# Where the first chunk's gate is held between its steps: SBUF in place of PSUM

## The chip, the cores and the metric

The kernel runs on one core of a Trainium2 chip. The metric is the device time of one execution in microseconds (us); the time of a kernel is the median of its timed runs. TensorE is called PE here (its weight loads PEld), VectorE is DVE, ScalarE is ACT, GpSimd is POOL, SyncE is SP. SBUF is the on-chip working memory, PSUM the memory that PE writes its results to; DVE and ACT reach both, POOL only SBUF.

## The reference

Sparse attention over 8 batches, 8 heads, 576 positions of 64 features, then a feed-forward layer of 4608 tokens (512 to 2048 to 512) with a quadratic gate.

```
scores = scale * q @ k.T; masked: heads 0-3 to the last 32 positions, heads 4-7 to a stride of 32
attn   = exp(scores - max); attn = attn / (attn.sum + 1e-9); x = attn @ v
h = x @ w_in                                 # 4608 x 2048
g = where(h >= 1, h, where(h <= -1, 0, (h + 1)**2 / 4))
out = g @ w_out                              # 4608 x 512
```

## The kernel before

The feed-forward layer goes over nine chunks `c` of 512 tokens, and in each chunk over 16 blocks `f` of 128 hidden features. For each block `up(c, f)` makes the hidden activations with 12 matmuls of 128x512 into one PSUM bank, the tile `h` (two such banks take turns). `gate(c, f)` turns them into the gate value g and splits it in two parts for the second product, a rounded high part `gh` and the remainder `gl`. `down(c, f)` multiplies both with the block's output weights, 12 matmuls into four PSUM banks. `down` of a block comes after the `up` of two blocks later, because gates wait in the list `pend`.

The gate is max(h, 1) or the square, whichever is smaller: ACT computes `u = relu(0.5 h + 0.5)` from PSUM into SBUF (L549), squares it in place (L550), DVE takes `min(max(h, 1), u)` (L554), then `gh` is a rounding copy of the result and `gl` the result minus `gh` (L559). In chunks 1 to 8 ACT makes `gh` (L556); in chunk 0 DVE makes it (L558). The tile `u` has one buffer, so L549 of a block has to wait until the block before has done with it.

Chunk 0 has much else to do at the same time. Weights arrive as 64-bit integers and are brought to floating point by all three engines: ACT `conv_a` (L178, L181), DVE `conv_b` (L186), POOL `conv_c` (L191), ACT `conv_d` (L197), and DVE `conv_e` (L201), which writes the low half of the weights. The attention of batch 1 is woven in between: `s` scores (PE L302), `m` masking (DVE L353), `x` row maximum (DVE L364), `a` subtraction (POOL L368), `e` exponential (ACT), `q` sum (DVE L379), `r` reciprocal (DVE L391) and scaling (POOL L392), `f` transposes (PE L405), `d` or `c` copy out of PSUM (L415, on DVE for `d`), `v` product with the values (PE L459), `h` and `l` into the feed-forward input (L500, L504).

The order on every engine is written out by hand (`manual_schedule`); nothing reorders it. For chunk 0 the table `STEPS` says what stands before `up`'s follow-up, before the gate, inside it (the call `between`) and behind it, and `halves` says which weight halves are converted around which gate: the conversion of (f + 2, 0), the input weights of two blocks later, and of the output weights of this block in the first gates.

```
STEPS = {2: ("s0", "", "m0 x0", "a0"), 3: ("s1", "e0 q0", "p0 m1 x1", "a1 r0"), 4: ("", "e1 q1", "p1", "r1"),
         5: ("f0", "", "d0", ""), 6: ("s2", "", "m2 x2", "a2"), 7: ("v0", "e2 q2", "p2 h0 l0", "r2"),
```

Of the kernel before, what the change touches and what calls it, by code (L numbers as in the profile page):

```python
# [23 lines left out]
def tile_sparse_attention_then_ffn(  # L24
# [518 lines left out]
    def gate(c, f, between=lambda: None):  # L543

        hp = o_ps.pop((c, f))
        gh = g_p.tile([P, CH], F32R, tag="gh", name=f"gh_{c}_{f}")
        gl = g_p.tile([P, CH], F32R, tag="gl", name=f"gl_{c}_{f}")
        u = g_p.tile([P, CH], F32, tag="u", bufs=1, name=f"u_{c}_{f}")
        nc.scalar.activation(u, hp, AF.Relu, bias=half, scale=0.5)  # L549
        nc.scalar.activation(u, u, AF.Square)  # L550
        between()

        g = u if (c, f) == (0, 0) else hp
        nc.vector.scalar_tensor_tensor(out=g, in0=hp, scalar=1.0, in1=u, op0=ALU.max, op1=ALU.min)  # L554
        if c:
            nc.scalar.copy(gh, g)  # L556
        else:
            nc.vector.tensor_copy(gh, g)  # L558
        nc.vector.tensor_tensor(out=gl, in0=g, in1=gh.bitcast(F32), op=ALU.subtract)  # L559
        return gh, gl  # L560
# [44 lines left out]
    with tc.manual_schedule():  # L605
# [36 lines left out]
        for c in range(NCH):  # L642
            b = need[c + 1] if c + 1 < NCH and need[c + 1] > need[c] else None
            go = attention(b, lambda u, kind, n: "a") if b is not None else None
            for f in range(NF):
                if c or f > 1:
                    up(c, f)
                pe, pre, mid, post = (LATER if c else STEPS).get(f, ("",) * 4) if b is not None else ("",) * 4
                if pe:
                    go(pe)  # L650
                if c == 0:
                    start_w(*halves[f])
                if pre:
                    go(pre)
                pend.append((c, f, gate(c, f, lambda: mid and go(mid))))
                if c == 0:
                    end_w(*halves[f])
                    if f == 9:
                        for i in range(2):
                            load_piece(NF - 2, i)  # L660
                        for i, k in ((0, 0), (0, 1), (1, 0)):
                            load_piece(NF - 1, i, k, o_p, "ob", 2)
                    if f == NF - 4:
                        load_piece(NF - 1, 1, 1, of=2)
                    if f == NF - 3:
                        fetch_qk(2, 0)
                if post:
                    go(post)
                n = 2 if 0 < c and (c, f) < (NCH - 1, NF - 1) else 1
                if len(pend) > 2:  # L670
                    down(*pend[:n])
                    del pend[:n]
# [61 lines left out]
```

## Time and profile before

| what | before |
|---|---|
| median of 3 timed runs | 881.38 us (881.37 to 883.25) |
| the profiled execution, its own time | 883.73 us |
| span of the profiled execution | 881.9 us |
| PE busy over the span | 872.9 us (99%) |
| PEld busy | 710.3 us (81%) |
| DVE busy | 384.6 us (44%) |
| ACT busy | 398.0 us (45%) |
| POOL busy | 114.7 us (13%) |

The profile comes from one execution. Its span runs from the first to the last recorded instruction; 1.8 us of the execution's own time lie outside of it. A busy share is an average over the whole span, and chunk 0 takes only its first part, so what the change does is read in that part.

### The profile page before, as it was taken

To read this page: it belongs to the slowest core of one execution; us is meant where nothing else is said; L and a number is where in the kernel's file an instruction comes from. 1 tells how busy PE (TensorE), PEld (TensorE's weight loads), DVE (VectorE), ACT (ScalarE), POOL (GpSimd) and SP (SyncE) were. 2 spreads that over 40 slices of the span, in tenths; PEclk is the share of its full clock that TensorE was granted. 3 is DMA by queue.
4 is the path that set the end of the run, shared out by engine and by line. 5 is a ranking of instruction groups with operands and counts; after the bars stand their busy time and mean duration, and the time that the engine had idled before them with its cause. 6 is when DMAs were issued, how large, how long until landed. Compare 5 with 4: busy or idle time off the path is not lost.

```text
span 881.9 us, 17353 instructions
## 1 busy us (share of the span) xinstructions
PE 872.9 (99%) x7253; PEld 710.3 (81%) x7253; DVE 384.6 (44%) x709; ACT 398.0 (45%) x732; POOL 114.7 (13%) x136
## 2 busy tenths in 40 slices
PE   8999999999999999999999999999999999999998
PEld 6788888888888888887888888888888888888886
DVE  5899854443453434434344345333453322222221
ACT  5889953434434443334434343444333433343333
POOL 6354411100120002100110011100210000000000
PEclk8999999999999999999999999999999999999999
DMA  9917331422232322421241223321222000000001
GB/s 354 405 65 242 114 121 61 140 59 60 105 100 81 83 70 72 125 64 62 81 145 52 67 105 94 87 82 49 76 82 60 33 29 1 0 35 14 1 0 48
DMA packets 41646, 77.61 MB, mean 88 GB/s; under 512 B 8800, under 2 KB 22112, under 8 KB 41568
## 3 DMA queue, kind: packets, MB, share of 16 engines
q1 hardware_dynamic: 41568, 76.50, 26.8%
q8 instruction: 57, 0.93, 0.4%
q14 instruction: 21, 0.17, 0.1%
HBM read 59.18 MB, written 17.30 MB: 87 GB/s over the span
## 4 chain that ended last, share of the span: by engine, by line
PE 95%; DMA 1%; ACT 1%; DVE 1%; SPq 1%; issue 0%; ACTq 0%; DVEq 0%
PE o L570 44%; PE h L540 44%; PE xp L459 3%; PE sc L302 3%; DMA qk<-in_qk_s 1%; PE tp L405 1%; SPq L443 0%; DMA pT<-there 0%; ACT u L549 0%; ACT u L550 0%; DMA there<-t 0%; DVE xTl L504 0%; DVE h L554 0%; SPq L237 0%; ACT gh L556 0%
## 5 line engine op out<-in xcount | busy, mean ns | idle before, releaser
L540 PE MATMUL h<-xTh,w 128*128 128x512 f32 x1152 | 373.2, 391 | 0.4 <-DVE u L554 0.4
L570 PE MATMUL o<-w,gh 128*128 128x512 f32 x1152 | 359.5, 393 | 0.1
L554 DVE SCALAR_TENSOR_TENSOR h<-h,u 128x512 f32<-128x512 f32 x143 | 100.0, 699 | 377.1 <-ACT u L550 377.0
L540 PEld LDWEIGHTS h<-xTh,w 128*128 128x128 f32 x1152 | 216.3, 188 | 46.6 <-DVE u L554 0.8
L570 PEld LDWEIGHTS o<-w,gh 128*128 128x128 f32 x1152 | 213.4, 188 | 45.3 <-ACT gh L556 0.6
L540 PE MATMUL h<-xTl,w 128*128 128x512 f32 x576 | 224.5, 390 | 0.4 <-DVE xTl L504 0.4
L570 PE MATMUL o<-w,gl 128*128 128x512 f32 x576 | 224.9, 390 | 0.0
L549 ACT ACTIVATE u<-h,half 128x512 f32<-128x512 f32 x144 | 99.1, 688 | 269.6 <-PE h L540 268.6
L559 DVE TENSOR_TENSOR gl<-h,gh 128x512 fp32r<-128x512 f32 x143 | 98.9, 692 | 84.6 <-ACT gh L556 83.7
L570 PEld LDWEIGHTS o<-w,gl 128*128 128x128 f32 x576 | 108.1, 188 | 25.7 <-DVE gl L559 0.6
L540 PEld LDWEIGHTS h<-xTl,w 128*128 128x128 f32 x576 | 108.1, 188 | 22.9 <-DVE xTl L504 1.1
L556 ACT CAST gh<-h 128x512 fp32r<-128x512 f32 x128 | 75.2, 587 | 100.1 <-DVE h L554 100.1
L550 ACT ACTIVATE u<-u 128x512 f32<-128x512 f32 x144 | 91.0, 632 | 4.6
L368 POOL TENSOR_TENSOR pr<-pr,st 128x768 f32<-128x768 f32 (+3 forms) x31 | 36.3, 1172 | 322.8 <-DVE st L364 307.6
L392 POOL TENSOR_TENSOR pr<-pr,st 128x648 f32<-128x648 f32 (+3 forms) x30 | 35.2, 1173 | 119.3 <-DVE st L391 118.4
L191 POOL TENSOR_TENSOR raw<-raw 128x512 uint32<-128x512 uint32 (+1 forms) x34 | 35.0, 1047 | 37.9 <-DVE raw L186 23.4
L504 DVE TENSOR_TENSOR xTl<-xp,xTh 128x216 fp32r<-128x216 f32 (+8 forms) x94 | 35.7, 442 | 6.0 <-ACT xTh L500 6.0
L383 ACT ACTIVATE st<-st 128x12 f32<-128x12 f32 (+2 forms) x32 | 6.8, 211 | 67.5 <-DVE st L379 67.4
L459 PEld LDWEIGHTS xp<-pT,v 64*64 64x64 f32 (+2 forms) x1760 | 29.0, 138 | 10.1 <-issue 8.2
L302 PEld LDWEIGHTS sc<-qk 64*32 64x32 f32 (+1 forms) x1856 | 25.9, 117 | 12.1 <-issue 10.1
L459 PE MATMUL xp<-pT,v 64*64 64x32 f32 (+2 forms) x1760 | 32.3, 224 | 1.5 <-DMA pT<-there 0.8
L500 ACT CAST xTh<-xp 128x216 fp32r<-128x216 f32 (+8 forms) x94 | 31.1, 459 | 6.0 <-DVE xTl L504 3.5
(56 smaller groups left out, 348.3 us busy)
## 6 DMA issues: line engine op xcount, KB each, us to landing
raw<-in_w SPq DMA_DIRECT2D x30, 512.0 KB, 9.6
qk<-in_qk_s SPq DMA_DIRECT2D x16, 604.0 KB, 4.9
qk<-in_qk_l SPq DMA_DIRECT2D x16, 576.0 KB, 4.8
out<-ob SPq DMA_DIRECT2D x35, 256.0 KB, 2.0
v<-in_v_l SPq DMA_DIRECT2D x21, 384.0 KB, 4.0
there<-t SPq DMA_DIRECT2D x96, 48.0 KB, 1.7
pT<-there SPq DMA_DIRECT2D x12, 384.0 KB, 3.0
v<-in_v_s SPq DMA_DIRECT2D x7, 384.0 KB, 4.4
```

The source lines that it names most:

```text
L302: nc.tensor.matmul(sc[j][i * Q:(i + 1) * Q, s, p], qk[:, 0, q0:q0 + Q], qk[:, 1, k0:k0 + W], start=u not in covered, stop=u not in covered)
L368: eng.tensor_tensor(out=pr, in0=pr, in1=st[:, 0].unsqueeze(2).broadcast_to(list(pr.shape)), op=ALU.add)
L392: eng.tensor_tensor(out=pr, in0=pr, in1=st[:, 2].unsqueeze(2).broadcast_to(list(pr.shape)), op=ALU.mult)
L459: nc.tensor.matmul(xp[p][j * D:(j + 1) * D, n], loaded[b, local, b0 + n][keys, j], qs, start=True, stop=True)
L504: nc.vector.tensor_tensor(out=dst[1], in0=src, in1=dst[0].bitcast(F32), op=ALU.subtract)
L540: nc.tensor.matmul(o_ps[c, f], wt[f][:, x, 0, cc * P:(cc + 1) * P], xT[y][:, cc, r0:r0 + CH], start=first and n == 0, stop=last and n == l ...
L549: nc.scalar.activation(u, hp, AF.Relu, bias=half, scale=0.5)
L550: nc.scalar.activation(u, u, AF.Square)
L554: nc.vector.scalar_tensor_tensor(out=g, in0=hp, scalar=1.0, in1=u, op0=ALU.max, op1=ALU.min)
L556: nc.scalar.copy(gh, g)
L559: nc.vector.tensor_tensor(out=gl, in0=g, in1=gh.bitcast(F32), op=ALU.subtract)
L570: nc.tensor.matmul(o_ps[c][t], gs[x][:, t * P:(t + 1) * P], wt[f][:, y, 1, :], start=f == 0 and n == 0, stop=f == NF - 1 and n == 2)
```

## The change

Only the place where L554 puts its result changes, and only in chunk 0. Before, block 0 alone kept the result in `u` in SBUF, and the other 15 blocks of chunk 0 wrote it back over `h` in PSUM, as all blocks of the later chunks do. After the change all 16 blocks of chunk 0 keep it in `u`. L558 and L559, which read the result, then read `u` in place of `h`.

```
-        g = u if (c, f) == (0, 0) else hp
+        g = hp if c else u
         nc.vector.scalar_tensor_tensor(out=g, in0=hp, scalar=1.0, in1=u, op0=ALU.max, op1=ALU.min)
         if c:
             nc.scalar.copy(gh, g)
         else:
             nc.vector.tensor_copy(gh, g)
         nc.vector.tensor_tensor(out=gl, in0=g, in1=gh.bitcast(F32), op=ALU.subtract)
```

No instruction is added, taken away or moved on any engine; the operands of 45 instructions on DVE differ. The rows below are DVE's order around the gate of block 2, before (-) and after (+); `h_2` is the PSUM bank of the block, `w` and `raw` are weights under conversion, `pr` and `st` belong to the attention.

```order
 L353 TENSOR_TENSOR pr_0_773<-sc_0_1_711,m_loc 128x384
 L364 TENSOR_REDUCE st_0_774<-pr_0_773 128x12
-L554 SCALAR_TENSOR_TENSOR h_2_697<-h_2_697,u_2_770 128x512
-L558 CAST gh_2_768<-h_2_697 128x512
-L559 TENSOR_TENSOR gl_2_769<-h_2_697,gh_2_768 128x512
+L554 SCALAR_TENSOR_TENSOR u_2_770<-h_2_697,u_2_770 128x512
+L558 CAST gh_2_768<-u_2_770 128x512
+L559 TENSOR_TENSOR gl_2_769<-u_2_770,gh_2_768 128x512
 L201 TENSOR_TENSOR w_781<-raw_190,w_781 128x512
 L201 TENSOR_TENSOR w_643<-raw_178,w_643 128x512
```

The cast and the subtraction lose their PSUM operand, and stay where they were. At the gate of block 5, which stands behind the copies of the transposes `tp` out of PSUM, it is the same; `pT` is their target.

```order
 L415 COPY pT_0_977<-tp_0_0_956 128x4x96
 L415 COPY pT_0_977<-tp_0_1_957 128x4x96
-L554 SCALAR_TENSOR_TENSOR h_5_943<-h_5_943,u_5_974 128x512
-L558 CAST gh_5_972<-h_5_943 128x512
-L559 TENSOR_TENSOR gl_5_973<-h_5_943,gh_5_972 128x512
+L554 SCALAR_TENSOR_TENSOR u_5_974<-h_5_943,u_5_974 128x512
+L558 CAST gh_5_972<-u_5_974 128x512
+L559 TENSOR_TENSOR gl_5_973<-u_5_974,gh_5_972 128x512
 L201 TENSOR_TENSOR w_983<-raw_667,w_983 128x512
 L201 TENSOR_TENSOR w_872<-raw_193,w_872 128x512
```

Two waits move with the operands: the bank `h` is free for PE after L554 instead of after L559, and `u` is free for the next block's L549 after L559 instead of after L554.

## Rows read from the trace of the kernel before

**Rows 1.** The page: the chain that ended last, share of the span by engine.

```profile
PE 95%; DMA 1%; ACT 1%; DVE 1%; SPq 1%; issue 0%; ACTq 0%; DVEq 0%
```

**Rows 2.** Windows: stretch, its length, busy us and instructions of each engine, granted clock, DMA.

```profile
32.44:124.00 91.56, 91.56 (x914) 74.38 (x918) 79.30 (x144) 76.87 (x145) 39.95 (x40) 1.00 0.48 170
124.00:881.90 757.90, 753.31 (x5808) 614.44 (x5796) 284.84 (x522) 301.59 (x542) 58.51 (x60) 1.00 0.22 66
```

**Rows 3.** What PE waited for, 32.5 to 124 us: us in total, times, longest.

```profile
PE h L540 <- DVE u L554: 0.4, 1, 0.4
```

**Rows 4.** DVE's groups by form, 0 to 125 us: busy us, mean ns, idle before.

```profile
L554 DVE SCALAR_TENSOR_TENSOR h<-h,u 128x512 f32<-128x512 f32 x16 | 11.1, 694 | 6.4 <-ACT u L550 6.3
L558 DVE CAST gh<-h 128x512 fp32r<-128x512 f32 x15 | 10.4, 692 | 0.9
L559 DVE TENSOR_TENSOR gl<-h,gh 128x512 fp32r<-128x512 f32 x15 | 10.4, 691 | 0.9
...
L559 DVE TENSOR_TENSOR gl<-u,gh 128x512 fp32r<-128x512 f32 x1 | 0.7, 692 | 0.0
L554 DVE SCALAR_TENSOR_TENSOR u<-h,u 128x512 f32<-128x512 f32 x1 | 0.7, 691 | 1.4 <-ACT u L550 1.4
...
L558 DVE CAST gh<-u 128x512 fp32r<-128x512 f32 x1 | 0.4, 426 | 0.0
```

**Rows 5.** POOL's timeline, 41 to 61 us: start, us, operation, count.

```profile
41.82 1.47 POOL L368 TENSOR_TENSOR pr<-pr,st 128x768 f32<-128x768 f32 x1 [0.16 <-DMA raw<-in_w]
...
48.10 0.83 POOL L368 TENSOR_TENSOR pr<-pr,st 128x384 f32<-128x384 f32 x1 [0.59 <-DVE st L364]
51.62 1.48 POOL L392 TENSOR_TENSOR pr<-pr,st 128x768 f32<-128x768 f32 x1 [2.69 <-DVE st L391]
53.05 2.22 POOL L191 TENSOR_TENSOR raw<-raw 128x512 uint32<-128x512 uint32 x2
...
58.28 2.22 POOL L191 TENSOR_TENSOR raw<-raw 128x512 uint32<-128x512 uint32 x2
```

**Rows 6.** DVE's timeline: the casts of blocks 2 to 5.

```profile
42.32 0.69 DVE L558 CAST gh<-h 128x512 fp32r<-128x512 f32 x1
...
48.72 0.69 DVE L558 CAST gh<-h 128x512 fp32r<-128x512 f32 x1
...
54.55 0.69 DVE L558 CAST gh<-h 128x512 fp32r<-128x512 f32 x1
...
60.24 0.69 DVE L558 CAST gh<-h 128x512 fp32r<-128x512 f32 x1
```

**Rows 7.** Timelines of DVE and POOL: an instruction of each, SBUF to SBUF, side by side.

```profile
76.91 1.51 DVE L186 TENSOR_SCALAR raw<-raw 128x512 uint32<-128x512 uint32 x1
...
76.86 1.28 POOL L392 TENSOR_TENSOR pr<-pr,st 128x648 f32<-128x648 f32 x1 [4.05 <-DVE st L391]
```

**Rows 8.** Timelines: what DVE makes, and the PE weight loads that use it or its banks.

```profile
50.05 1.28 DVE L201 TENSOR_TENSOR w<-raw,w 128x512 fp32r<-128x512 f32 x2
55.95 1.28 DVE L201 TENSOR_TENSOR w<-raw,w 128x512 fp32r<-128x512 f32 x2
58.53 1.01 DVE L415 COPY pT<-tp 128x384 f32<-128x384 f32 x2
...
51.41 0.41 PEld L540 LDWEIGHTS h<-xTh,w 128*128 128x128 f32 x2
53.67 0.81 PEld L405 LDWEIGHTS tp<-ident,pr 128*128 128x128 f32 x6
57.54 0.41 PEld L540 LDWEIGHTS h<-xTh,w 128*128 128x128 f32 x2
60.12 0.61 PEld L302 LDWEIGHTS sc<-qk 64*64 64x64 f32 x35 [0.35 <-issue]
```

**Rows 9.** Timelines of DVE and ACT: a block's L559 and the next block's L549.

```profile
49.44 0.69 DVE L559 TENSOR_TENSOR gl<-h,gh 128x512 fp32r<-128x512 f32 x1
...
50.75 0.68 ACT L549 ACTIVATE u<-h,half 128x512 f32<-128x512 f32 x1
```

More of the change, by code (lines that the diff above doesn't have):

```diff
@@ L551, in gate @@
         between()
-        g = u if (c, f) == (0, 0) else hp
+        g = hp if c else u
         nc.vector.scalar_tensor_tensor(out=g, in0=hp, scalar=1.0, in1=u, op0=ALU.max, op1=ALU.min)
```

## The prediction

> **What bounds the kernel now.** I read the chain that ended last first, since it says which engine the end hangs on: PE holds 95% of it, DVE 1% [rows 1]. Then the busy time by stretch, to see whether that also holds where the change is. The first changed instruction stands behind the gate of block 1, after 32.44 us, and the last is done before 124 us. In this stretch PE is busy for 91.56 us out of 91.56, at full granted clock [rows 2]. The list of PE's waits has one entry there, 0.4 us for L554, which is block 0's own gate just at its start, and block 0 is not changed [rows 3]. So from 32.44 to 124 us there is no idle time of PE that a faster DVE could take away. DVE is busy for 79.30 us of the same stretch and POOL for 39.95 [rows 2]: both are heavily loaded, neither sets the end, but both feed PE and could come too late.
>
> **The change part by part.** Fifteen blocks change, three instructions each. Block 0 has always used the new form, so the trace of before holds one of each and the prices need no guess.
>
> L554 takes 694 ns into PSUM and 691 into SBUF: nothing (15 x 3 ns). L559 takes 691 ns with one operand in PSUM and 692 with both in SBUF: nothing, while POOL is idle, as it was beside block 0's. L558 takes 692 ns from PSUM and 426 ns from SBUF [rows 4]. Fifteen casts by 0.266 us are 4.0 us less work on DVE. That is the lower end of what DVE can gain or lose: -4.0 us, if no cast is disturbed.
>
> It will be disturbed. A DVE operation from SBUF to SBUF with one input does not run beside a POOL operation: L186, starting at 76.91 while POOL was at work from 76.86 to 78.14 (76.86 + 1.28), took 1.51 us and ended at 78.42, 0.28 us behind POOL [rows 7]. The old cast does not care: the one at 54.55 took 0.69 us in the middle of POOL's pair that ran from 53.05 to 55.27 [rows 5, 6]. I take the new cast to behave like L186, since both go from SBUF to SBUF and a free one takes little over 0.4 us. Then it ends 0.28 us behind the POOL operation that it meets. Block by block, at the times of before:
>
> - Block 2: POOL ends at 43.29, the cast at 43.57 in place of 43.01: +0.56.
> - Block 3: POOL ends at 48.93, the cast at 49.21 in place of 49.41: -0.20.
> - Block 4: POOL ends at 55.27, the cast at 55.55 in place of 55.24: +0.31.
> - Block 5: POOL ends at 60.50, the cast at 60.78 in place of 60.93: -0.15 [rows 5, 6].
>
> Read the same way, the casts of blocks 1, 6, 8, 9, 11 and 13 also start beside a POOL operation (ten of fifteen), and those of 7, 10, 12, 14 and 15 do not and gain 0.27 each. The ten go from -0.24 to +0.60 apiece, and the sum over all fifteen is about nothing: five gains of 0.27 against a net loss of some 1.4 us. So DVE's 4.0 us are mostly given back to POOL, and what is left is a small shift back and forth.
>
> **Does the shift reach PE?** Between the gates of blocks 2 and 5 DVE has no pause, so I carry it on. It is +0.56 behind block 2. POOL's L368 of block 3 waits for DVE and moves along, so there the cast starts at 49.28, POOL ends at 49.49 and the cast at 49.77 in place of 49.41: +0.36. Block 4: start 54.91, POOL's pair now ends at 55.63, the cast at 55.91 in place of 55.24: +0.67. Four uses by PE stand close behind [rows 5, 8]:
>
> - The low weights of block 5: L201's first one ends near 50.74, with 0.36 at 51.10; PE loads them at 51.41. Spare 0.31.
> - The transposes: POOL's L392 ends at 53.10, then 53.46; PE starts at 53.67. Spare 0.21.
> - The low weights of block 6: 56.64, then 57.31; PE at 57.54. Spare 0.23.
> - The scores of block 6 go into the banks that L415 empties: 59.54, then 60.21; PE at 60.12. Late by 0.1.
>
> So PE may lose a tenth or two at 60 us, and something like it once or twice more where attention banks change hands. Each such loss pushes PE back and gives the next use more room. I take 0.2 us in sum; the bounds are 0 and, if the losses above came three times over, 0.6.
>
> Two waits move. The bank `h` comes free 1.4 us earlier, after L554 in place of L559 (0.69 + 0.69 us behind it); PE did not wait for it, so this gives nothing, but it takes out a wait that a late DVE would have run into. The buffer `u` comes free 1.4 us later. Block 4's L549 starts at 50.75, and L559 of block 3 ends at 50.13 [rows 9]: 0.62 to spare, 0.26 with the shift of 0.36. Behind L549 on ACT stand the square and the casts of the next weight halves (L197), for which DVE's L201 and then PE wait.
>
> The sum is made against the profiled execution, 883.73 us by its own time with a span of 881.9: 883.7 + 0.2 = 883.9. That execution is 2.35 us above the median of the timed runs, 881.38, and one of those is at 883.25, so against the median it is 881.6.
>
> **The rivals.**
>
> *ACT is held up by `u`.* If the shift passes such a gap as the 0.62 us behind block 3, L549 waits for L559 and takes the rest of ACT's queue with it. That lag then meets L197, L201 and PE's loads, where 0.2 to 0.9 us are to spare [rows 8]. Some three such places at 0.3 us each: 882.5 us. For it: ACT is busy for 76.87 of the 91.56 us [rows 2]. Against it: PE loads block 3's `gh` at 54.45, 4.3 us after its L559 has ended [rows 9], so a late gate alone costs nothing.
>
> *Slower: the subtraction waits too.* L559 now has both inputs in SBUF. If such an instruction also can't run beside POOL, it waits behind whichever POOL operation starts first. In blocks 1 to 5 that would be one more L191 of some 1.04 us each, 5.2 us by the scores at 60 us; DVE has no pause to take it up, and 0.5 us of room remain: PE loses 4.7 us, 886.1 in all. It decides once DVE is late by over about 3 us. For it: nothing in the rows, since no subtraction of this form met POOL in them. Against it: behind the cast of block 3 POOL's next operation starts at 51.62, 1.5 us after L559's end at 50.13 [rows 5, 9], and behind blocks 2, 4 and 5 it is alike. So even if the mechanism is real, it strikes at most in blocks 11 and 13.
>
> The Trainium skill (SBUF — State Buffer, Who interferes with whom) says that a DVE instruction with two SBUF inputs does contend with a POOL instruction that reads SBUF, the later of the two waiting in full. By that rule the sum above would gain 0.6 us at each of blocks 11 and 13 on DVE, and PE's time would stay within a few tenths of mine; by block 0's row alone it gains nothing.
>
> *Faster: the 4.0 us reach the end.* It would be 877.4 us, if the casts ran undisturbed and PE were waiting for them in a way its rows hide. Against it: PE's busy time fills the stretch to the last hundredth, and block 3's cast ends 5 us before PE loads its result [rows 2, 6, 9].
>
> *The change does nothing at all on DVE* (the cast stays at 0.69 us): excluded for a free one by block 0's 426 ns, and it would give 881.4 us.
>
> **How the numbers follow.** A timed difference under 0.3%, 2.6 us, can't be told from none here; the timed runs of before spread over 1.9 us by themselves. Forecast (PE loses 0 to 0.6 us) 0.84; ACT held up by `u` 0.08; DVE's cast unchanged 0.02; subtraction or casts hold up PE by over 2.6 us 0.04; faster 0.02. The first three all lie within 0.3%: 0.94. The range goes from 880.8, half a microsecond under the fastest run of before, to 883.6, which takes in its slowest run and the 0.2 us.
>
> **What would show it.** Right: L558 in chunk 0 at 0.43 us in the five free blocks and 0.5 to 1.3 us in the ten others; the ends of such casts 0.28 us behind POOL's; DVE's busy time in the stretch within 2 us of 79.3; PE's idle time there below 0.6 us, with its waits, if any, on L415, L504, L201 or POOL's L392. Wrong: several waits of PE, or one over 1 us; L559 at over 0.7 us in many blocks; L549 waiting for L559. If the time behind the stretch changes by over 1 us, something that I have not looked at is at work.

## The result and the profile after

The changed kernel takes 882.95 us (median of 19 runs, 881.54 to 885.42) against 881.38 us (19 runs, 880.84 to 883.59). The ratio is 1.0016, 95% interval 1.0009 to 1.0024: within 0.3%, but not nothing; it is slower. Over all kernels here about one run in four shows a mean granted clock of 0.997 or less and takes some 2 us longer, so the means below are over the other runs.

The profiled execution after the change has a span of 882.6 us and an own time of 884.55. First the page's first lines, after and before:

```profile
span 882.6 us, 17361 instructions
PE 873.4 (99%) x7253; PEld 710.5 (81%) x7253; DVE 385.8 (44%) x709; ACT 398.1 (45%) x732; POOL 114.9 (13%) x136
```

```profile
span 881.9 us, 17353 instructions
PE 872.9 (99%) x7253; PEld 710.3 (81%) x7253; DVE 384.6 (44%) x709; ACT 398.0 (45%) x732; POOL 114.7 (13%) x136
```

The counts of DVE, ACT, POOL and PE are as before, yet there are eight rows more. They are waits, which the page doesn't count as an engine's work; the source view of L554 after the change names them, on DVE's queue (`DVEq`):

```profile
L554 DVE SCALAR_TENSOR_TENSOR u<-h,u x16: 674/682/692, 31.7 to 119.7; 128x512 f32<-128x512 f32 x16
L554 DVEq EVENT_SEMAPHORE  x8: 21/21/21, 34.0 to 116.9; - x8
```

So "no instruction is added" in the part on the change is true of the operations, not of the waits: in eight blocks L554, which now writes `u`, has a wait more, and it stands on a row of its own. It is a wait for DVE itself: the eight rows wait on the semaphore that L554 raises, and in the trace only DVE's instructions raise it. This turns out to matter.

DVE's groups after, 0 to 126 us, which answer to [rows 4]:

```profile
L559 DVE TENSOR_TENSOR gl<-u,gh 128x512 fp32r<-128x512 f32 x16 | 13.0, 814 | 1.0
L554 DVE SCALAR_TENSOR_TENSOR u<-h,u 128x512 f32<-128x512 f32 x16 | 11.0, 685 | 4.4 <-ACT u L550 4.3
L558 DVE CAST gh<-u 128x512 fp32r<-128x512 f32 x16 | 9.9, 618 | 1.0
```

These groups take in block 0, which has not changed. Over the fifteen other blocks the casts gained 0.06 us on average and not 0.27, and the subtractions lost 0.13. DVE is busy for 80.38 us in the stretch of [rows 2], 1.08 more than before. The timelines show where, DVE's casts of blocks 2, 3, 4, 5, 6 and 8, the subtraction of block 8, and POOL beside them [rows 5, 6]:

```profile
42.19 1.27 DVE L558 CAST gh<-u 128x512 fp32r<-128x512 f32 x1
...
49.16 0.50 DVE L558 CAST gh<-u 128x512 fp32r<-128x512 f32 x1
...
54.79 1.02 DVE L558 CAST gh<-u 128x512 fp32r<-128x512 f32 x1
...
60.75 0.61 DVE L558 CAST gh<-u 128x512 fp32r<-128x512 f32 x1
...
67.45 1.25 DVE L558 CAST gh<-u 128x512 fp32r<-128x512 f32 x1
...
79.85 0.48 DVE L558 CAST gh<-u 128x512 fp32r<-128x512 f32 x1
80.43 1.34 DVE L559 TENSOR_TENSOR gl<-u,gh 128x512 fp32r<-128x512 f32 x1
```

```profile
41.70 1.47 POOL L368 TENSOR_TENSOR pr<-pr,st 128x768 f32<-128x768 f32 x1 [0.17 <-DMA raw<-in_w]
...
53.31 2.22 POOL L191 TENSOR_TENSOR raw<-raw 128x512 uint32<-128x512 uint32 x2
...
67.14 1.27 POOL L368 TENSOR_TENSOR pr<-pr,st 128x648 f32<-128x648 f32 x1
...
78.82 2.41 POOL L191 TENSOR_TENSOR raw<-raw 128x512 uint32<-128x512 uint32 x2
```

The cast at 42.19 ends at 43.46, 0.29 us behind POOL's operation (41.70 + 1.47 = 43.17); the one at 67.45 ends at 68.70, 0.29 behind 68.41. In block 8 the cast starts beside the first of POOL's two additions, which ends at 80.05, and ends 0.28 behind it at 80.33, while the second addition is already running. Then the subtraction has to wait for the second: 1.34 us, ending 0.54 behind POOL. Blocks 11 and 13 show the same 1.34.

PE now waits in chunk 0. These are its weight loads' waits from 30 to 135 us, less two rows of the kind "issue", in which they waited for nothing that the profile shows. The first was there before (it is the 0.4 of [rows 3] as the loads see it):

```profile
...
PEld h L540 <- DVE u L554: 0.8, 1, 0.8
PEld tp L405 <- POOL raw L191: 0.4, 1, 0.4
PEld sc L302 <- DVE u L554: 0.4, 1, 0.4
PEld sc L302 <- DVE pT L415: 0.4, 1, 0.4
PEld tp L405 <- DVE xTl L504: 0.2, 1, 0.2
```

The chain that ended last puts a size on it. It shows the start of block 2's `up` and the start of the attention's first value product of batch 2, in chunk 1, before and after:

```profile
32.44 3.02 PE h L540 x12
...
168.49 1.53 PE xp L459 x96
```

```profile
32.45 3.01 PE h L540 x12
...
168.94 1.53 PE xp L459 x96
```

136.05 us lie between the two before, 136.49 after: PE is 0.44 us late when it leaves chunk 0. Nearly all of it comes from one place, the transposes of block 8, whose loads stood at 73.52 without a pause before (first fence) and now wait for the banks that L504 empties (second fence):

```profile
73.52 0.48 PEld L405 LDWEIGHTS tp<-ident,pr 128*128 128x128 f32 x3
```

```profile
73.96 0.20 PEld L405 LDWEIGHTS tp<-ident,pr 128*128 128x128 f32 x2 [0.42 <-POOL raw L191]
74.37 0.14 PEld L405 LDWEIGHTS tp<-ident,pr 128*128 128x128 f32 x1 [0.20 <-DVE xTl L504]
```

The first of these two rows names POOL's L191, which writes none of its operands (`tp`, `ident`, `pr`) and ended at 73.81. The wait row just before it is on DVE's semaphore and ended at 73.94, when the first L504 of the pair was done (73.85).

The second loss is far behind the change. In the later chunks the transposed probabilities go through memory: eight writes (L443) and, when they have landed, one read back (L444). SyncE's timeline at 488 us, before and after:

```profile
484.98 3.61 SPq L443 DMA_DIRECT2D there<-t  x8
489.87 0.52 SPq L444 DMA_DIRECT2D pT<-there  x1
```

```profile
485.02 3.61 SPq L443 DMA_DIRECT2D there<-t  x8
490.90 0.52 SPq L444 DMA_DIRECT2D pT<-there  x1
```

From the first write to the read it is 4.89 us before and 5.88 after. The DMA view of 488.2 to 490.5 us shows the last write landing after 1.6 us before, and no queue but that of the data (first fence). After the change it shows a transfer on another queue there, and the last write landing after 2.6 us (second fence):

```profile
q1 hardware_dynamic: 230, 0.12, 24.2%
...
there<-t SPq DMA_DIRECT2D x1, 40.0 KB, 1.6
```

```profile
q14 instruction: 1, 0.01, 1.6%
...
there<-t SPq DMA_DIRECT2D x1, 40.0 KB, 2.6
```

It is a load of code, 8 KB. PE, which made these 88 products without a pause before (first fence), waits for the read back behind the first 48 (second fence):

```profile
492.90 1.51 PE L459 MATMUL xp<-pT,v 64*64 64x32 f32 x88
```

```profile
492.95 0.90 PE L459 MATMUL xp<-pT,v 64*64 64x32 f32 x48
494.40 0.81 PE L459 MATMUL xp<-pT,v 54*64 54x64 f32 x40 [0.55 <-DMA pT<-there]
```

### The profile page after: what moved, and what is told of

Its sections match the earlier page's. It is cut to its first block, busy times and chain, and to the rows that moved or that the text cites. A ratio compares the mean times of both kernels' runs of the same rounds, so it can differ in the third digit from the quotient of the medians.

```text
span 882.6 us, 17361 instructions
## 1 busy us (share of the span) xinstructions
PE 873.4 (99%) x7253; PEld 710.5 (81%) x7253; DVE 385.8 (44%) x709; ACT 398.1 (45%) x732; POOL 114.9 (13%) x136
## 4 chain that ended last, share of the span: by engine, by line
PE 95%; DMA 2%; ACT 1%; DVE 1%; SPq 1%; issue 0%; POOL 0%; ACTq 0%; DVEq 0%
PE o L570 44%; PE h L540 44%; PE xp L459 4%; PE sc L302 3%; DMA pT<-there 1%; SPq L443 1%; PE tp L405 1%; DMA qk<-in_qk_l 1%; DMA there<-t 0%; DMA v<-in_v_s 0%; ACT pr L375 0%; DVE xTl L504 0%; POOL pr L368 0%; ACT u L549 0%; DVE t L429 0%
## 5 line engine op out<-in xcount | busy, mean ns | idle before, releaser
L554 DVE SCALAR_TENSOR_TENSOR h<-h,u 128x512 f32<-128x512 f32 x128 | 89.6, 700 | 374.3 <-ACT u L550 374.3
L549 ACT ACTIVATE u<-h,half 128x512 f32<-128x512 f32 x144 | 99.0, 687 | 269.3 <-PE h L540 268.3
L559 DVE TENSOR_TENSOR gl<-h,gh 128x512 fp32r<-128x512 f32 x128 | 88.6, 692 | 83.7 <-ACT gh L556 83.7
L191 POOL TENSOR_TENSOR raw<-raw 128x512 uint32<-128x512 uint32 (+1 forms) x34 | 35.4, 1058 | 39.4 <-DVE raw L186 22.7
L504 DVE TENSOR_TENSOR xTl<-xp,xTh 128x216 fp32r<-128x216 f32 (+8 forms) x94 | 35.7, 442 | 5.9 <-ACT xTh L500 5.3
```

What stands on the lines that cost most here:

```text
L191: nc.gpsimd.tensor_tensor(out=H_, in0=H_, in1=L, op=ALU.add)
L504: nc.vector.tensor_tensor(out=dst[1], in0=src, in1=dst[0].bitcast(F32), op=ALU.subtract)
```

## The experiments

Two theories at first. A: what the change costs, it costs through the lateness of PE in chunk 0. C: there is a cost of its own behind chunk 0. B is chance. G came out of the traces: the eight waits move a load of DVE's code onto the write at 488 us. D, E, F and H are told in the expectations that name them. In the table "late" is the time from block 2's `up` to that value product of batch 2, less the 136.05 us of before; "write" is the time from the first of the eight writes to the read at 488 us; the mean difference is against the runs of before on the same chip, with its standard error from the spread of the runs on both sides.

| kernel | ratio, 95% interval | mean difference, us (runs) | late, us | write, us |
|---|---|---|---|---|
| before, again | 1.0005, 0.9995 to 1.0015 | -0.06 +- 0.14 (8) | 0.06 | 4.88 |
| changed, again | 1.0010, 1.0001 to 1.0019 | +0.92 +- 0.20 (9) | 0.43 | 5.64 |
| free blocks only | 1.0005, 0.9996 to 1.0014 | -0.04 +- 0.13 (9) | 0.04 | 4.88 |
| the other blocks only | 1.0014, 1.0004 to 1.0025 | +0.90 +- 0.16 (7) | 0.51 | 4.89 |
| PE late by 2 matmuls | 1.0010, 0.9999 to 1.0020 | +0.51 +- 0.25 (7) | 0.47 | 4.89 |
| PE late by 4 matmuls | 1.0015, 1.0004 to 1.0025 | +1.25 +- 0.17 (9) | 0.90 | 4.89 |
| changed, block 6 in PSUM | 1.0015, 1.0003 to 1.0027 | +0.57 +- 0.21 (8) | 0.05 | 5.99 |
| before, 8 idle instructions | 1.0009, 1.0001 to 1.0018 | +0.95 +- 0.13 (11) | 0.00 | 5.66 |
| changed, 16 of them | 1.0006, 0.9997 to 1.0016 | +0.44 +- 0.22 (9) | 0.43 | 4.86 |
| block 6 in PSUM, 16 | 1.0001, 0.9993 to 1.0010 | +0.12 +- 0.18 (9) | 0.06 | 4.87 |
| before, 16 | 1.0006, 0.9995 to 1.0017 | +0.26 +- 0.26 (7) | 0.00 | 4.87 |

**The kernel before, once more.** No edit.

> The kernel before, unchanged, as a control. Theory A (what the change costs, it costs in chunk 0, where PE waits some 0.45 us in the profile after): ratio 1.000, PE busy throughout 32.5 to 124 us. Rival B (the measured 1.4 us comes from the runs' own spread and not from the change): this control moves by 0.5 us or more as well.

It does not move: -0.06 us. B falls.

**The changed kernel, once more.** No edit.

> The changed kernel, unchanged. Theory A: PE's idle time and waits in 32.5 to 124 us as in the first profile of it, about 0.45 us, and the ratio near 1.0005, some 0.5 us. Rival B: a ratio that wanders between 1.000 and 1.002. Rival C (the cost lies behind chunk 0, where PE waits for attention transfers): the ratio stays near 1.0016, and PE's waits for pT from there add up to 0.5 us or more above those of the control.

The lateness in chunk 0 comes back to the hundredth, 0.43, and PE's loads wait at the same four places. The time is 0.92 us over before, about twice the lateness; the first runs, by their ratio, gave 1.4. The late write is there again, but in this trace PE doesn't wait for its read, and its waits for `pT` behind chunk 0 come to 0.2 us against 0.5 in the control. So C's second sign is not there. This trace is of the fastest of the eleven runs (881.69 us).

**Only the blocks whose cast is free.**

```
-        g = hp if c else u
+        g = u if not c and f in (0, 7, 10, 12, 14, 15) else hp
```

> Only the blocks whose cast met no POOL operation (7, 10, 12, 14, 15, and 0 as before) keep the gate in SBUF. Theory A: five casts at 0.43 us, DVE's busy time 1.3 us less than before, no wait of PE in 32.5 to 124 us, ratio 1.000. Rival D (the SBUF form costs by itself, wherever it stands): ratio about a third of the whole change's, 1.0005.

Five casts at 427 ns, no wait of PE, no lateness, no cost: -0.04 us. The SBUF form is not dear by itself. It is not a gain either: the casts' 1.3 us were not wanted.

**Only the others.**

```
-        g = hp if c else u
+        g = hp if c or f in (7, 10, 12, 14, 15) else u
```

> The other ten blocks (1 to 6, 8, 9, 11, 13) and 0 keep it in SBUF. Theory A: all of the change's cost is here: casts of 0.45 to 1.3 us, three subtractions at 1.34 us, PE 0.4 to 0.6 us late by 124 us, ratio as for the whole change or a little above. Rival D: two thirds of it.

The lateness is 0.51 us and the cost +0.90 +- 0.16: as much as the change's, so what it costs comes with the blocks whose cast meets POOL. Two subtractions take 1.34 us, in blocks 8 and 13, and not three; in block 11 it is the cast that waits, 1.11 us. This kernel has three rows more than before and its write at 488 us is on time, so 0.4 us of its cost have no place that its one trace shows. In that trace even the lateness is mostly taken up, at a read back 394 us into the span.

**PE late by itself**, with two and with four matmuls more.

```
+        extra = 2 if (c, f) == (0, 8) else 0
+        todo = [todo[0]] * extra + todo
...
-                             start=first and n == 0, stop=last and n == len(todo) - 1)
+                             start=first and n <= extra, stop=n < extra or last and n == len(todo) - 1)
```

> The kernel before, with the first matmul of block 8's up issued two times more in chunk 0, each time as a closed group that the next one overwrites: PE is 2 x 0.227 = 0.45 us late from there on, as it is in the changed kernel, with nothing altered on DVE. Theory A (lateness of PE in chunk 0 counts one for one): 0.45 us slower than before, ratio 1.0005. Rival C (being late at that place costs as much again behind chunk 0): 0.9 us, ratio 1.0010, as the changed kernel.

> The same with four extra matmuls, 0.91 us of PE. Theory A: 0.9 us, ratio 1.0010. Rival C: 1.4 us or more.

They cost 0.51 +- 0.25 us for 0.47 and 1.25 +- 0.17 for 0.90. Lateness counts about one for one, perhaps a little more with four. But the trace with four also has a late write far behind, at 676 us: 5.92 us from the first write to the read, against 4.89 before, with a load of code on queue 8 beside it and a wait of PE of 0.4 us. The 0.92 us of the changed kernel lie between the two, though it is only as late as the first; the errors are too wide for this alone to decide.

**Block 6 put back to PSUM.**

```
-        g = hp if c else u
+        g = hp if c or f == 6 else u
```

> The changed kernel with block 6 alone put back to PSUM; its cast was the one that met POOL's subtraction at 67 us and took 1.25 us. Theory A: PE's wait before the transposes at 74 us goes (0.4 of the 0.45 us), what is left by 124 us is under 0.1 us, and the ratio falls to 1.000. Rival E (the lateness is the sum of many small ones): PE loses 0.3 us or more still.

The transposes of block 8 stand without a pause again (the loads of this kernel, whose start is 1.2 us earlier), and the lateness falls from 0.44 to 0.05 us:

```profile
72.38 0.48 PEld L405 LDWEIGHTS tp<-ident,pr 128*128 128x128 f32 x3
```

So the wait's cause is the one cast of block 6, which ended 1.0 us later than before with the shift that it inherited. But the expected ratio of 1.000 did not come: +0.57 +- 0.21 us with hardly any lateness to explain it. A alone falls here. The write at 488 us is late in this trace too, 5.99 us, and this kernel has the same eight waits. That is where G came from: in the traces of the changed kernel, its repeat and this one the load of code on queue 14 starts 1.0 to 1.4 us behind the last of the eight writes; in the traces of before, free blocks, others and PE late it starts 8.1 to 9.1 us behind it. (Queue 14 has another load there, about 6 us behind the write in every kernel; that one doesn't move.)

**Without POOL's additions.**

```
             conv_b(f, i)
-            conv_c(f, i)
```

> The changed kernel without POOL's additions of the weight halves in the loop (L191), which leaves the low bits out of most weights. Theory A (the casts are stretched by POOL's operations alone): the casts of blocks 1, 4, 5, 8, 11 and 13, which met these additions, at 0.43 us, all subtractions at 0.69 us, and only those of blocks 2, 3, 6 and 9 that meet the attention's subtraction still at 0.5 to 1.3 us. Rival F (the SBUF form is slower in a loaded stretch for another reason): they stay above 0.5 us.

This kernel was timed once, so it has no row in the table. As expected by A: DVE's casts of blocks 1 to 6 in its timeline (L558 is L557 here). Blocks 1, 4 and 5 are free now, 2, 3 and 6 still meet the attention's subtraction, and the mean of all subtractions is 693 ns, none held up:

```profile
34.82 0.43 DVE L557 CAST gh<-u 128x512 fp32r<-128x512 f32 x1
40.40 1.27 DVE L557 CAST gh<-u 128x512 fp32r<-128x512 f32 x1
47.37 0.50 DVE L557 CAST gh<-u 128x512 fp32r<-128x512 f32 x1
53.01 0.43 DVE L557 CAST gh<-u 128x512 fp32r<-128x512 f32 x1
58.37 0.43 DVE L557 CAST gh<-u 128x512 fp32r<-128x512 f32 x1
64.04 1.02 DVE L557 CAST gh<-u 128x512 fp32r<-128x512 f32 x1
```

**Idle instructions on DVE**, one or two behind each of the first eight gates of chunk 1: in the kernel before (8, and 16), in the changed one (16), and in the one with block 6 back (16).

```
+    spare = const.tile([P, 1], F32, name="spare")
...
                 pend.append((c, f, gate(c, f, lambda: mid and go(mid))))
+                if c == 1 and f < 8:
+                    for _ in range(1):
+                        nc.vector.memset(spare, 0.0)
```

> The kernel before with eight idle instructions on DVE in chunk 1 (memsets of one column, one behind each of the first eight gates), where DVE has time to spare. In the profile of the changed kernel DVE has eight more rows, all waits, and a load of its code then falls 1.0 us behind the last write of the transposed probabilities at 488 us in place of 8.1 us; that write lands 1 us later and PE waits 0.6 us. Theory G (what the change costs behind chunk 0 is this shift of a code load): here the load moves to within 1.5 us of that write, the write takes 2.4 us or more in place of 1.6, PE waits at 490 us, and the time rises by 0.5 us with nothing altered in the gate. Rival H (the late write in the changed kernel is chance or comes from the gate): no wait of PE at 490 us, ratio 1.000.

> The changed kernel with sixteen such instructions, two behind each gate, which should move that code load to before the write's start. Theory G: the late write at 488 us goes, what is left is the 0.45 us of chunk 0, ratio 1.0005, about 0.4 us faster than the changed kernel, unless another code load now meets another such write. Rival H: unchanged, ratio 1.0010 to 1.0016.

> The changed kernel with block 6 alone in PSUM, which took PE's wait at 74 us away, and with the sixteen instructions. Theory G with theory A: both costs gone, ratio 1.000, time as before. Rival H: ratio 1.0010, as the kernel with block 6 put back had 1.0015.

> The kernel before with the sixteen instructions, as a control of them: DVE's idle time in chunk 1 takes them up, and no code load meets the write at 488 us. Theory G: ratio 1.000; if it is slower, the profile shows another write late.

The times of all four go the way that G says, and the loads and writes at 488 us do too; what G doesn't give is the size in the first. Eight idle instructions in the kernel before move the load to 1.0 us behind the last write; SyncE's timeline and the DMA view of 486.1 to 488.4 us of this kernel, in which L443 and L444 are one line further down, read like those of the changed one:

```profile
482.91 3.61 SPq L444 DMA_DIRECT2D there<-t  x8
488.57 0.52 SPq L445 DMA_DIRECT2D pT<-there  x1
```

```profile
q14 instruction: 1, 0.01, 1.2%
...
there<-t SPq DMA_DIRECT2D x1, 40.0 KB, 2.4
```

Nothing of its gate is changed, PE is not late in chunk 0, and it costs 0.95 +- 0.13 us, as much as the change itself. So H falls. But G expected 0.5 us, and in this trace PE loses only 0.4 us at that read. The other half has no place: the eight rows move the other loads of DVE's code too, by 7 to 11 us in this trace, and whether one of them costs something in other executions was not tested. With sixteen, in the changed kernel, the load starts 3.1 us ahead of the last write, the write is on time, and what is left is 0.44 +- 0.22 us, the lateness of chunk 0. With block 6 back as well it is 0.12 +- 0.18: both causes out, nothing left that can be told from none. What the sixteen take off is 0.48 +- 0.30 in the changed kernel and 0.45 +- 0.28 with block 6 back: each alone is under two standard errors, the two together a little over two. The control, before with sixteen, is at 0.26 +- 0.26. Its write at 488 us is on time, the one at 390 us is no later than before (5.94 us to the read against 6.25), and its trace shows no loss.

## Why the prediction was right or wrong

The forecast, no difference of over 0.3%, was right, and the time lies in the range. The sum was not: it gave 0.2 us over before, at most 0.6, and the change costs 0.9 us by its second set of runs and 1.4 by the first (ratio 1.0016). Only 0.44 of that is where I looked. That the time still falls inside is owed to the width of the range, which goes up to the slowest run of before; as far as the part behind chunk 0 goes, it was luck.

*The casts and POOL*: right, and to a tenth of a microsecond. Carried forward, the casts of blocks 3 and 4 were to end at 49.77 and 55.91 us; they end at 49.66 and 55.81. Without POOL's additions the ones that met them are free, which shows the cause. Four of the ten that meet POOL become longer than the 0.69 us of before (blocks 2, 4, 6 and 9); the other six come out at 0.44 to 0.61. The +0.60 at the top of the ten, which by the rows is block 8's, was read wrong: its cast waits only for the addition beside which it starts. And the ten shifts, added up again from the trace of before, make a net loss of 1.2 us and not 1.4, which changes nothing.

*The subtraction*: the prediction gave it two blocks at most, 11 and 13; there are three, 8 being the third, at 1.34 us each. The cast waits for the first of two POOL operations and leaves the subtraction behind it to wait for the second. This form met no POOL operation in the trace of before, and the rule of the Trainium skill (SBUF — State Buffer, Who interferes with whom) that two SBUF inputs contend with a POOL instruction that reads SBUF agrees with these rows: 0.65 us more each, where the sum by it had 0.6 at two blocks. It cost PE nothing that the waits show.

*What reaches PE*: the mechanism was right, the term mis-sized, 0.44 us against 0.2. The scores of block 6, which the working had late by 0.1, cost under 0.1. The weights of blocks 5 and 6 and the transposes of block 5 were in time, as worked out. What I passed over as "once or twice more where attention banks change hands" was the transposes of block 8: I had carried the shift only to block 5, and block 6's +0.55 came on top of it just ahead of the L504 pair that frees their banks. Putting that one block back takes the wait away.

*The row of before that was missing*: PE's load of block 3's `gh`, named for 54.45 us with [rows 9], is not among those rows. It is this one:

```profile
54.45 0.30 PEld L570 LDWEIGHTS o<-w,gh 128*128 128x128 f32 x2
```

*ACT held up by `u`*: it did not happen. L549 waits for L559 nowhere after the change; the least room between them in chunk 0 is 0.6 us.

*What fell outside*: the step that failed is "the change part by part", where three instructions a block were counted and the waits were not. Eight waits more on DVE move its later code by eight rows, and a load of that code meets the last of eight small writes some 400 us later. In the first trace the write lands 1 us late where PE has less than that to spare. Eight idle instructions in the kernel before move the load and the write in the same way; with sixteen in the changed one the write is on time again. The prediction's last sentence on what would make it wrong, a change of time behind the stretch, allowed for this with 1 us, and the single traces show less than that (by the end the profiled execution after is 0.6 us behind that of before, counted from block 2's `up`).

Open: the two costs don't add up. The changed kernel has both and costs about as much as the eight idle instructions alone. In its trace a wait of PE for another read back, at 394 us, is 0.4 us in place of 0.8, and PE's lateness falls there from 0.44 us to 0.04; it does the same in the traces of its repeat and of the ten blocks only, but not in that of the changed kernel with sixteen. PE's waits from 385 to 402 us, before (first fence) and after (second fence):

```profile
PE xp L459 <- DMA pT<-there: 0.8, 1, 0.8
```

```profile
PE xp L459 <- DMA pT<-there: 0.4, 1, 0.4
```

By the end PE is 0.6 us late in the first trace of the changed kernel, 0.2 in its repeat, 0.3 with the ten blocks only and 0.5 with the eight idle instructions. Those are single executions, and all four show less than the mean times do; where the rest is lost is not known.

## What to carry to other kernels

A faster form of an instruction is worth only what the engine that sets the end was waiting for; here PE waited for nothing, and all that the faster cast could do to the time was to come late, because it can't run beside POOL's operations as the slower form did. Carry such a shift forward through every block until the engine has a pause, and hold it against each bank that changes hands, not only against the first few uses. When two traces differ far from the edit, compare the counts of rows, waits included, and look at where the loads of code fall: eight idle instructions are a cheap control for that.

## What the runs showed of the hardware

A DVE cast from SBUF to SBUF (0.43 us when free) that starts beside a POOL operation ends 0.28 to 0.29 us behind it; a subtraction with both inputs in SBUF takes 1.34 us in place of 0.69. The cast that reads PSUM takes 0.69 us beside POOL as well as alone.

A load of code of 8 KB that starts 1.0 to 1.4 us behind a small write on another DMA queue delays it: 2.4 to 2.7 us to landing in place of 1.6. PE doesn't always pay for it: in one of four such traces it had the room. Where the load falls hangs on the count of all rows of the engine, waits included: eight rows of DVE moved it from 8.1 us behind the write to 1.0. The Trainium skill (Runtime: NRT & Kernel Launch, Instruction fetch mechanics) says that an engine's sequencer fetches its code through its own DMA queue, in blocks of 16 KiB. The traces agree in that code comes on other queues, 8 and 14, than the data on queue 1. They differ in the rest: the loads on queue 14 are of 8 KB (21 in 0.17 MB), and of its two loads near 488 us only one moves with DVE's rows, so that this queue seems to carry the code of more than one engine.

In eight blocks a wait of L554 for earlier work of DVE itself stands on a row of its own, 21 ns each; nothing in the list of operations shows it.
